# Two cached-attention decodes: spreading the query broadcast over the heads, loading one weight later, and turning the output projections round

## Chip, cores, metric

One core of one Trainium2 chip. The metric is the device time of one execution in microseconds (us); times quoted for a kernel are medians of its runs. A ratio is the mean time of one kernel's fast runs over that of the other's in the same rounds, so it is not quite the ratio of the medians. The kernel before has runs near 883.5 and runs near 886.3 and little between; why, I don't know, and 3 us of any comparison with it are worth no more than that. Differences between two variants are therefore read off their own medians (each was always timed beside the kernel before, on one chip per session).

## The reference

```python
# twice: A with all 16384 keys, B with the last W = 4096 keys
q = (x @ wq).reshape(B, Sq, 32, 128)            # x: 1 x 1 x 512
scores = einsum("bhqd,bhkd->bhqk", q, k) * 128 ** -0.5
o = einsum("bhqk,bhkd->bhqd", softmax(scores), v)
out = o.reshape(B, Sq, 4096) @ wo               # wo: 4096 x 512
# result: concatenate([a, b], axis=-1): 1 x 1 x 1024, bf16
```

One query, 32 heads of 128, each with its own K and V: 352 MB are read and each number is used once.

## The kernel before

Heads alternate: A0, B0, A1, B1, ... (A head i is `hh` = 2i, B head i is `hh` = 2i + 1). K streams through a ring of five slots on the SP queue, V through a ring of four on the ACT queue; a head of A takes two slots, one of B half of one. For A, PE transposes K in groups of eight tiles, ACT copies each group to SBUF, PE multiplies it with q. For B, DVE multiplies K with a q broadcast over all partitions (`qb_sb`) and sums. Both take exp on ACT; PE then multiplies with V, one head later (`ov`).

```python
# SP: a slot is loaded again when its last user is done
if seq[phh][0] == "A": sp.wait_ge(pe_tr, gstart_u[pu] + ugroups[pu])
else:                  sp.wait_ge(dve_red, b_rank[phh] + 1)
...
if hh == WOA_AFTER_HEAD:                        # 6
    sp.wait_ge(pe_q, 1 + 8)                     # all qb batches made: wbuf is free
    sp.dma_start(wo_view[:, :, :], A_wo.rearrange("(c p) n -> p c n", p=128)).then_inc(s_w, 16)

# PE at head 2: broadcast q of B for all heads, eight batches through one PSUM bank
for bch in range(8):
    if bch >= 1: pe.wait_ge(dve_m, DM_QB0 + bch - 1)
    ...  # 16 matmuls of 128 columns into misc7
# DVE: the eight copies stand ahead of its head loop
for bch in range(8):
    v.wait_ge(pe_q, 2 + bch)
    v.tensor_copy(qb_sb[:, bch * 4 * DH : (bch + 1) * 4 * DH], misc7[:, 0 : 4 * DH]).then_inc(dve_m, 1)
for hh in range(NH):
    if hh == last_a_hh + 1: a_final_dve()       # A's tail, ahead of B head 31
    ...

# ACT at a B head: the exp stands ahead of the next A head's copies
act.wait_ge(dve_red, hb + 1)

# PE, the end: 32 matmuls of N = 512 for each branch (b_final likewise, with wob_view)
for h in range(HQ):
    last = pe.matmul(outA_ps, onorm[:, h : h + 1], wo_view[:, h, :], start=(h == 0), stop=(h == HQ - 1))
```

`wo_view` shares its SBUF buffer with wq, so A_wo can only be loaded when the last qb batch is made. B_wo goes into two slots of the K ring, when K is done with them. Both are read as `(c p) n -> p c n`: 32 pieces of 1 KB to a partition, 4096 in all.

The softmax here doesn't subtract the row's maximum and nothing guards it: scores larger than these inputs give would overflow.

## Time and profile before

| | |
|---|---|
| time | 886.31 us, median of the first 6 runs |
| span of the profiled run | 884.8 us |
| bytes read | 352.32 MB, 398 GB/s over the span |
| busy share | PE 73%, weight loads 64%, ACT 56%, DVE 25% |

No engine is near full; the table alone doesn't say what binds. The row of GB/s does: it stands near 424 in most slices. So I kept one ledger: add up, over stretches of 5 us, how much of each stretch the DMA would not have needed at 424 GB/s. A stretch at 212 GB/s has lost 2.5 us. The prediction shows the lines for the kernel before.

### The profile page before, as it was taken

The numbers are of one execution on the slowest core, as the hardware profiler recorded it, in microseconds if no ns is written. First come the engines' busy times: TensorE is split into PE (matmuls) and PEld (weight loads), VectorE is DVE, ScalarE is ACT, GpSimd is POOL, SyncE is SP. The second block draws the span as 40 slices with busy tenths as digits, with TensorE's granted clock in tenths as the row PEclk, the third lists the DMA queues.
The fourth block names the chain that finished last, engine by engine and source line by source line (L and its number), as shares of the span: only waits on it lengthen the run. The fifth ranks groups of instructions, "written<-read, shape, count | busy, mean of one in ns | idle before, by whom it ended". The sixth has DMA issues, their size and how long they took to land.

```text
span 884.8 us, 29291 instructions
## 1 busy us (share of the span) xinstructions
PE 647.1 (73%) x13764; PEld 568.8 (64%) x13764; DVE 223.9 (25%) x87; ACT 498.2 (56%) x641; POOL 0.7 (0%) x6
## 2 busy tenths in 40 slices
PE   0776983687777778777777787777777877767788
PEld 0666872576666667666666676766666766666673
DVE  0016300633321133333211333333112333332003
ACT  0514771575555676655555776555556775555560
POOL 0000000000000000000000000000000000000000
PEclk9955885687667788776678788666688777667788
DMA  8997899999999999999999999999999999999990
GB/s 339 423 428 313 348 408 401 428 423 423 423 426 423 426 423 424 420 417 422 410 425 410 414 426 424 424 414 419 418 419 424 411 416 424 423 408 420 403 337 6
DMA packets 38202, 354.21 MB, mean 400 GB/s; under 512 B 4289, under 2 KB 12481, under 8 KB 12482
## 3 DMA queue, kind: packets, MB, share of 16 engines
q1 hardware_dynamic: 24258, 184.56, 50.8%
q10 hardware_dynamic: 13824, 167.78, 45.1%
q8 instruction: 108, 1.77, 0.8%
q14 instruction: 12, 0.10, 0.0%
HBM read 352.32 MB, written 0.00 MB: 398 GB/s over the span
## 4 chain that ended last, share of the span: by engine, by line
DMA 71%; PE 14%; another core or an unknown queue 7%; DVE 3%; ACT 3%; issue 1%; SPq 1%; ACTq 0%; DVEq 0%
DMA vring<-in_A_v_cache_dram 68%; PE ol L506 7%; DMA kring<-in_A_k_cache_dram 3%; ACT kts L392 3%; PE ktp L470 2%; PE misc L453 2%; DVE sbb L334 2%; PE misc L535 1%; PE misc L557 1%; DVE prd L325 1%; PE sba L486 1%; DVE qb_sb L294 1%; DMA kring<-in_B_k_cache_dram 1%; SPq L214 1%
## 5 line engine op out<-in xcount | busy, mean ns | idle before, releaser
L392 ACT ACTIVATE kts<-ktp 128x1024 bf16<-128x1024 bf16 x512 | 475.0, 1078 | 35.1 <-PE ktp L470 34.5
L470 PE MATMUL ktp<-ident,kring 128*128 128x128 bf16 x4096 | 361.1, 245 | 19.8 <-DMA kring<-in_A_k_cache_dram 19.7
L470 PEld LDWEIGHTS ktp<-ident,kring 128*128 128x128 bf16 x4096 | 285.8, 111 | 21.3 <-DMA kring<-in_A_k_cache_dram 18.4
L486 PE MATMUL sba<-qT_sb,kts 128*128 128x1 bf16 x4096 | 183.2, 166 | 70.6 <-ACT kts L392 42.7
L506 PE MATMUL ol<-ebuf,vring 128*128 128x1 bf16 x5120 | 149.7, 165 | 112.2 <-DMA vring<-in_A_v_cache_dram 107.9
L486 PEld LDWEIGHTS sba<-qT_sb,kts 128*128 128x128 bf16 x4096 | 149.2, 99 | 128.0 <-ACT kts L392 126.8
L506 PEld LDWEIGHTS ol<-ebuf,vring 128*128 128x128 bf16 x5120 | 142.5, 103 | 116.4 <-DMA vring<-in_A_v_cache_dram 110.1
L325 DVE TENSOR_TENSOR prd<-kring,qb_sb 128x4096 bf16<-128x4096 bf16 x32 | 73.3, 2292 | 539.3 <-DMA kring<-in_B_k_cache_dram 539.1
L417 ACT ACTIVATE ebuf<-sbb 128x32 bf16<-128x32 f32 x32 | 7.3, 229 | 319.2 <-PE ol L514 248.1
L334 DVE TENSOR_REDUCE sbb<-prd 128x32 f32<-128x4096 bf16 x32 | 141.4, 4420 | 1.1
L432 PE MATMUL misc<-xT_sb,wbuf 128*128 128x1 bf16 x128 | 3.6, 165 | 25.3 <-DMA wbuf<-in_A_wq_dram 25.3
L432 PEld LDWEIGHTS misc<-xT_sb,wbuf 128*128 128x128 bf16 x128 | 3.5, 104 | 25.3 <-issue 25.3
L453 PE MATMUL misc<-wbuf,xrep 128*128 128x128 bf16 x128 | 15.1, 312 | 5.5 <-DVE qb_sb L294 5.5
L453 PEld LDWEIGHTS misc<-wbuf,xrep 128*128 128x128 bf16 x128 | 13.0, 146 | 7.4 <-DVE qb_sb L294 7.4
L402 ACT ACTIVATE ebuf<-sba 128x128 bf16<-128x128 f32 x32 | 8.9, 277 | 14.4 <-PE sba L486 14.4
L294 DVE CAST qb_sb<-misc 128x512 bf16<-128x512 f32 x8 | 5.5, 692 | 37.2 <-PE misc L453 37.2
L514 PE MATMUL ol<-rowsum,ones_col 128*1 128x1 f32 x128 | 12.1, 164 | 0.0
L300 DVE RECIPROCAL linv<-ol 1x32 f32<-1x32 f32 x1 | 0.3, 346 | 39.9 <-PE ol L514 39.9
L535 PE MATMUL misc<-wbuf,onorm 128*1 128x512 bf16 x32 | 9.7, 478 | 0.5 <-DVE onorm L308 0.5
L557 PE MATMUL misc<-kring,onorm 128*1 128x512 bf16 x32 | 8.8, 442 | 0.5 <-DVE onorm L351 0.5
L535 PEld LDWEIGHTS misc<-wbuf,onorm 128*1 128x1 bf16 x32 | 3.1, 100 | 6.8 <-issue 3.9
L557 PEld LDWEIGHTS misc<-kring,onorm 128*1 128x1 bf16 x32 | 2.9, 94 | 5.9 <-issue 2.5
(25 smaller groups left out, 25.1 us busy)
## 6 DMA issues: line engine op xcount, KB each, us to landing
vring<-in_A_v_cache_dram ACTq DMA_DIRECT2D x64, 2048.0 KB, 23.1
kring<-in_A_k_cache_dram SPq DMA_DIRECT2D x64, 2048.0 KB, 25.1
kring<-in_B_k_cache_dram SPq DMA_DIRECT2D x32, 1024.0 KB, 18.6
vring<-in_B_v_cache_dram ACTq DMA_DIRECT2D x32, 1024.0 KB, 16.4
wbuf<-in_A_wq_dram SPq DMA_DIRECT2D x1, 4096.0 KB, 19.7
wbuf<-in_B_wq_dram SPq DMA_DIRECT2D x1, 4096.0 KB, 20.9
wbuf<-in_A_wo_dram SPq DMA_DIRECT2D x1, 4096.0 KB, 61.7
kring<-in_B_wo_dram SPq DMA_DIRECT2D x1, 4096.0 KB, 37.0
```

The source lines that it names most:

```text
L294: v.tensor_copy(qb_sb[:, bch * 4 * DH : (bch + 1) * 4 * DH], misc7[:, 0 : 4 * DH],).then_inc(dve_m, 1)
L325: v.tensor_tensor(PRD[:, :].rearrange("p (c d) -> p c d", d=DH), Kring[:, ks * UC : ks * UC + TB, :], qb_bcast(hb), op=ALU.mult,).then_inc ...
L334: v.tensor_reduce(SBB[hb % 2][:, 0:TB], PRD[:, :].rearrange("p (c d) -> p c d", d=DH), AXX, ALU.add,).then_inc(dve_red, 1)
L392: act.activation(KTs[g % NS][:, 0 : GS * 128], KTP[g % NKB][:, 0 : GS * 128], ACTF.Copy,).then_inc(act_ev, 1)
L402: act.activation(Ebuf[e][:, 0:TA], SBA[:, 0:TA], ACTF.Exp, bias=0.0, scale=inv_sqrt_dh, accum_out=rowsum[e][:, 0:1],).then_inc(act_ex, 1)
L453: last = pe.matmul(misc7[:, i * DH : (i + 1) * DH], xrep[:, jc, :], wq_view[:, jc, hb * DH : (hb + 1) * DH], start=(jc == 0), stop=(jc == ...
L470: last = pe.transpose(KTP[g % NKB][:, t * 128 : (t + 1) * 128], Kring[:, ks * UC + c, :], ident[:, :],)
L486: last = pe.matmul(SBA[:, c0 + c : c0 + c + 1], KTs[g % NS][:, t * 128 : (t + 1) * 128], qT_sb[:, a_rank[hh] : a_rank[hh] + 1], start=True ...
L506: pe.matmul(OL[b][:, hidx : hidx + 1], Vring[:, vs * UC + c, :], Ebuf[e][:, c0 + c : c0 + c + 1], start=first, stop=(c0 + c == T - 1),)
L514: pe.matmul(OL[b][0:1, HQ + hidx : HQ + hidx + 1], ones_col[:, 0:1], rowsum[e][:, 0:1], start=True, stop=True,).then_inc(pe_ov, 1)
L535: last = pe.matmul(outA_ps, onorm[:, h : h + 1], wo_view[:, h, :], start=(h == 0), stop=(h == HQ - 1),)
L557: last = pe.matmul(outB_ps, onorm[:, HQ + h : HQ + h + 1], wob_view[:, h, :], start=(h == 0), stop=(h == HQ - 1),)
```

## The change

Its intent: keep the start from stopping (the qb batches spread over heads 2, 4, ... 16, their copies put where they are needed), and shorten the serial end (128 matmuls of N = 1 in place of 32 of N = 512, for each branch). A_wo has to be loaded later for the first; A's tail on DVE goes behind B head 31 for the second.

```diff
-            WOA_AFTER_HEAD = 6
+            WOA_AFTER_HEAD = 24
 # DVE
-                for bch in range(8):
+                def qb_copy(bch):
...
                 for hh in range(NH):
-                    if hh == last_a_hh + 1:
-                        a_final_dve()
...
+                    if hb == 0:
+                        qb_copy(0)
+                    if 3 <= hb <= 9:
+                        qb_copy(hb - 2)
...
-                if NH <= last_a_hh + 1:
-                    a_final_dve()
+                a_final_dve()
...
-                v.tensor_copy(out_sb[0:1, 0:D], outA_ps).then_inc(dve_m, 1)
                 v.wait_ge(pe_fin, 4)
-                v.tensor_copy(out_sb[0:1, D : 2 * D], outB_ps).then_inc(
+                v.tensor_copy(out_colsb[:, 0:8], outcol_ps).then_inc(dve_m, 1)
+                v.wait_ge(pe_fin, 5)
+                v.tensor_copy(out_rowsb[0:8, 0:128], outrow_ps).then_inc(
 # PE
-                    if hh == 2:
-                        qb_batches()
+                    if hh >= 2 and hh % 2 == 0 and hh // 2 <= 8:
+                        qb_batches(hh // 2 - 1)
...
-                    for h in range(HQ):
-                        last = pe.matmul(
-                            outA_ps,
-                            onorm[:, h : h + 1],
-                            wo_view[:, h, :],
+                    for nb in range(4):
+                        for h in range(HQ):
+                            last = pe.matmul(
+                                outcol_ps[:, nb : nb + 1],
+                                wo_view[:, h, nb * 128 : (nb + 1) * 128],
+                                onorm[:, h : h + 1],
... # the same for B, then
+                    pe.wait_ge(dve_m, DM_OUTCOL)
+                    pe.transpose(outrow_ps, out_colsb[:, 0:8], ident[:, :]).then_inc(
```

The output is then stored as 8 rows of 256 B in place of one of 2 KB.

More of the change, by code (lines that the diff above doesn't have):

```diff
@@ L141, in bass_concat_heads__gqa_block_cached__sliding_block_cached__decode_kernel @@
         onorm = sbuf("onorm", [128, 2 * HQ], BF16)
-        out_sb = sbuf("out_sb", [1, 2 * D], BF16)
+        out_colsb = sbuf("out_colsb", [128, 8], BF16)
+        out_rowsb = sbuf("out_rowsb", [8, 128], BF16)
         wq_view = wbuf[:, :].rearrange("p (jc n) -> p jc n", jc=NJ)
@@ L159, in bass_concat_heads__gqa_block_cached__sliding_block_cached__decode_kernel @@
         qT_ps = misc6[:, 0:HQ]
-        outA_ps = misc6[0:1, 0:512]
-        outB_ps = misc7[0:1, 0:512]
+        outcol_ps = misc6[:, 0:8]
+        outrow_ps = misc7[:, :].bitcast(BF16)[0:8, 0:128]
         s_x = sem("s_x")
@@ L188, in bass_concat_heads__gqa_block_cached__sliding_block_cached__decode_kernel @@
         DM_ONORMB = 21
-        DM_OUTA = 22
-        DM_OUTB = 23
+        DM_OUTCOL = 22
+        DM_OUTROW = 23
         with nc.Block() as block:
@@ L270, in _ @@
                 ).then_inc(s_w, 16)
-                sp.wait_ge(dve_m, DM_OUTB)
+                sp.wait_ge(dve_m, DM_OUTROW)
                 sp.dma_start(
-                    out[0, 0:1, 0 : 2 * D],
-                    out_sb[0:1, 0 : 2 * D],
+                    out[0, 0, 0 : 2 * D].rearrange("(r c) -> r c", c=128),
+                    out_rowsb[0:8, 0:128],
                 ).then_inc(s_out, 16)
@@ L356, in _ @@
                 ).then_inc(dve_m, 1)
-                v.wait_ge(pe_fin, 2)
-                v.tensor_copy(out_sb[0:1, 0:D], outA_ps).then_inc(dve_m, 1)
                 v.wait_ge(pe_fin, 4)
-                v.tensor_copy(out_sb[0:1, D : 2 * D], outB_ps).then_inc(
+                v.tensor_copy(out_colsb[:, 0:8], outcol_ps).then_inc(dve_m, 1)
+                v.wait_ge(pe_fin, 5)
+                v.tensor_copy(out_rowsb[0:8, 0:128], outrow_ps).then_inc(
                     dve_m, 1
@@ L427, in _, with qT_A_block, qb_batches @@
             def _(pe):
-                pe.wait_ge(s_x, 16 * 2 * NJ)
-                pe.wait_ge(s_w, 16)
-                for ha in range(HQ):
-                    for jc in range(NJ):
-                        ins = pe.matmul(
-                            qT_ps[:, ha : ha + 1],
-                            wq_view[:, jc, ha * DH : (ha + 1) * DH],
-                            xT_sb[:, jc : jc + 1],
-                            start=(jc == 0),
-                            stop=(jc == NJ - 1),
-                        )
-                ins.then_inc(pe_q, 1)
+                def qT_A_block():
+                    pe.wait_ge(s_x, 16 * 2 * NJ)
+                    pe.wait_ge(s_w, 16)
+                    last = None
+                    for ha in range(HQ):
+                        for jc in range(NJ):
+                            last = pe.matmul(
+                                qT_ps[:, ha : ha + 1],
+                                wq_view[:, jc, ha * DH : (ha + 1) * DH],
+                                xT_sb[:, jc : jc + 1],
+                                start=(jc == 0),
+                                stop=(jc == NJ - 1),
+                            )
+                    last.then_inc(pe_q, 1)
+                    pe.wait_ge(dve_m, DM_QTA)
+                qT_A_block()
                 pe.wait_ge(gps, 2)
-                pe.wait_ge(dve_m, DM_QTA)
-                def qb_batches():
+                def qb_batches(b0):
                     pe.wait_ge(s_w, 32)
                     pe.wait_ge(dve_m, DM_XREP)
-                    for bch in range(8):
+                    for bch in range(b0, b0 + 1):
                         if bch >= 1:
@@ L533, in a_final @@
                     last = None
-                    for h in range(HQ):
-                        last = pe.matmul(
-                            outA_ps,
-                            onorm[:, h : h + 1],
-                            wo_view[:, h, :],
-                            start=(h == 0),
-                            stop=(h == HQ - 1),
-                        )
+                    for nb in range(4):
+                        for h in range(HQ):
+                            last = pe.matmul(
+                                outcol_ps[:, nb : nb + 1],
+                                wo_view[:, h, nb * 128 : (nb + 1) * 128],
+                                onorm[:, h : h + 1],
+                                start=(h == 0),
+                                stop=(h == HQ - 1),
+                            )
                     last.then_inc(pe_fin, 1)
@@ L555, in b_final @@
                     last = None
-                    for h in range(HQ):
-                        last = pe.matmul(
-                            outB_ps,
-                            onorm[:, HQ + h : HQ + h + 1],
-                            wob_view[:, h, :],
-                            start=(h == 0),
-                            stop=(h == HQ - 1),
-                        )
+                    for nb in range(4):
+                        for h in range(HQ):
+                            last = pe.matmul(
+                                outcol_ps[:, 4 + nb : 5 + nb],
+                                wob_view[:, h, nb * 128 : (nb + 1) * 128],
+                                onorm[:, HQ + h : HQ + h + 1],
+                                start=(h == 0),
+                                stop=(h == HQ - 1),
+                            )
                     last.then_inc(pe_fin, 1)
+                    pe.wait_ge(dve_m, DM_OUTCOL)
+                    pe.transpose(outrow_ps, out_colsb[:, 0:8], ident[:, :]).then_inc(
+                        pe_fin, 1
+                    )
                 lag = []
```

## The prediction

> **What bounds the kernel now.** I read the page's slices first, then the stretches in which the DMA share falls, then the timeline of the end, and only then the groups and waits. The slices' last two rows:
>
> ```profile
> DMA  8997899999999999999999999999999999999990
> GB/s 339 423 428 313 348 408 401 428 423 423 423 426 423 426 423 424 420 417 422 410 425 410 414 426 424 424 414 419 418 419 424 411 416 424 423 408 420 403 337 6
> HBM read 352.32 MB, written 0.00 MB: 398 GB/s over the span
> ```
>
> Each slice is 884.8 / 40 = 22.1 us. From slice 7 to slice 37 the core reads 403 to 428 GB/s with its DMA engines busy: the bound there is the bytes. At 421 GB/s, 352.3 MB take 837 us, so about 48 us of the span are not full DMA time. They lie in slices 3 and 4 (66 to 110 us), in the last two slices, and a little at the very start. Time saved in the middle on PE, ACT or DVE is worth nothing; time saved in those places is worth its full length, if nothing else then lets the DMA run dry.
>
> The hole near the start, by stretches (us, then busy time and count of PE, PEld, DVE, ACT, POOL, clock, DMA share, GB/s):
>
> ```profile
> 70.00:75.00 5.00, 3.68 (x35) 3.41 (x32) 3.81 (x3) 0.00 (x0) 0.00 (x0) 0.50 1.02 434
> 75.00:80.00 5.00, 0.17 (x6) 0.18 (x7) 4.87 (x2) 1.46 (x4) 0.00 (x0) 0.50 0.44 147
> 80.00:85.00 5.00, 5.00 (x79) 5.00 (x77) 4.97 (x2) 5.00 (x6) 0.00 (x0) 0.50 0.87 370
> 85.00:90.00 5.00, 4.73 (x100) 4.06 (x97) 0.38 (x1) 4.96 (x7) 0.00 (x0) 0.96 0.61 215
> 90.00:95.00 5.00, 3.58 (x92) 2.99 (x91) 4.82 (x2) 4.10 (x7) 0.00 (x0) 1.00 0.46 131
> 95.00:100.00 5.00, 5.00 (x146) 4.95 (x145) 1.89 (x1) 0.68 (x3) 0.00 (x0) 0.57 0.98 419
> ```
>
> From 75 to 95 us the core read (147 + 370 + 215 + 131) x 5 us = 4.32 MB, which is 10.2 us at 425 GB/s: **9.8 us are lost**. Why it ran dry stands in the timeline of the SP queue (start and duration, us; the issue is held for 34.6 us) and then in the chain that ended last:
>
> ```profile
> 44.24 34.62 SPq L234 DMA_DIRECT2D kring<-in_A_k_cache_dram  x2
> ```
>
> ```profile
> 71.77 2.29 DVE prd L325
> 74.08 4.43 DVE sbb L334
> 78.77 1.01 ACT kts L392
> ```
>
> The second of these two K loads needs the slot of B head 0, which is free only when DVE has reduced it (78.5 us). DVE reduces it only after all eight qb copies, because they stand ahead of the head loop; PE makes the eight batches in one lump from 50.5 to 71 us, 2.67 us each (1.9 matmul, 0.7 copy). ACT also waits there, its exp of B head 0 standing ahead of head 2's evictions; so the SP queue and the V loads both stop.
>
> The end, in the timeline:
>
> ```profile
> 860.07 0.35 DVE L300 RECIPROCAL linv<-ol 1x32 f32<-1x32 f32 x1 [39.91 <-PE ol L514]
> 861.61 9.75 PE L535 MATMUL misc<-wbuf,onorm 128*1 128x512 bf16 x32 [0.51 <-DVE onorm L308]
> 871.29 0.95 PE L506 MATMUL ol<-ebuf,vring 128*128 128x1 bf16 x32
> 872.40 0.35 DVE L343 RECIPROCAL linv<-ol 1x32 f32<-1x32 f32 x1 [4.18 <-PE ol L514]
> 873.72 8.75 PE L557 MATMUL misc<-kring,onorm 128*1 128x512 bf16 x32 [0.51 <-DVE onorm L351]
> 882.51 0.68 DVE L360 CAST out_sb<-misc 1x512 bf16<-1x512 f32 x1 [8.26 <-PE misc L557]
> 883.21 0.32 SPq L272 DMA_DIRECT2D out_dram<-out_sb  x1
> ```
>
> From 860 us to the end it is one serial chain with no DMA left to hide behind. The two output projections are 18.5 of its 24.7 us.
>
> **What the Trainium skill says.** (1) "DMA: Bandwidth & Descriptors", section "Issuing engines are not separate DMA queues": loads issued from SP and ACT run on the same 16 engines. The trace agrees: both queues are active, yet the sum stays near 424 GB/s. (2) "TensorE: Matmul & The Clock Gate", section "Back-to-back issue gap": a matmul of N=512 follows the last after N/1.2 ns cold, N/2.4 + 2.5 ns warm (427 and 216); the section before it puts a floor of about 25 ns on any matmul, however small N is. In the trace the weight loads of line 535 start 0.42 to 0.43 us apart while the clock is 0.50, so that agrees; and the N=1 matmuls, each with its own 128-column weight load, come at 149.7 us / 5120 = 29.2 ns, near the floor. (3) The first page's "Specifications" say that below 512 B the DMA does a read-modify-write. The new output store has 256 B rows; no row of this trace shows what eight of them cost.
>
> **The change, part by part.**
>
> 1. *qb batches spread over heads 2, 4, ... 16, with the copies moved into DVE's loop.* Same count of instructions; it moves them. Only batch 0 stays ahead of B head 0: PE has it at 52.4 us, the copy ends at 53.1, product and sum take 2.3 + 4.4 us, so B head 0 is reduced at 60.0 instead of 78.5. The stopped K load leaves at 60 instead of 78.9. I follow the issues on. Head 2's first K unit lands at 58.1 (issued 29.35, 28.7 us), so its evictions start at 60 and free its slot about 66.8 (6.6 us later, as before): one more 1 MiB load. Its second unit lands near 68 and is done near 75: 2 MiB of K, then 1 MiB of V for head 3. B head 1 (landed 73.4) is reduced at about 80.1: 2 MiB of K. The V units of head 4 follow near 78 and 81: 4 MiB. Before, 29 MiB had been issued when the DMA ran dry at 76. Now 3 MiB more are in by 67, good to 83.5 us at 2.5 us per MiB; and 9 MiB more are in by 81, good to about 106. After that PE and ACT need about 23 us a pair of heads against the DMA's 25.1 us, so the queues stay filled. Gain: the whole 9.8 us, less some residue: **9.5 us**. The later batches add 1.9 us to PE in eight pairs of heads, in a stretch where PE waits for V anyway: 0.
>
> 2. *A_wo loaded after head 24 instead of 6.* It must move, since wq's buffer is now in use until head 16. Same 4 MiB, same 1 KB pieces. Before, it took 61.7 us to land and held K back until PE stood still (140 to 160 us), yet the DMA stayed at 420 to 424 GB/s there, with one dip to 360 in 130 to 140 (1.5 us). The same should happen near 300 us: 0.
>
> 3. *Projections with wo as the stationary operand.* Each 32 matmuls of N=512 become 4 x 32 = 128 of N=1. 128 x 29.2 ns = 3.74 us against 9.75 and 8.75. Gain 6.0 + 5.0 = **11.0 us**, all on the chain. The next wait below is B_wo, issued at 828.0 with 37.0 us to landing, so at 865.0. The new chain is at its B projection at 861.61 + 3.74 + 0.95 + about 1.4 = 867.7: 2.7 us to spare.
>
> 4. *New end.* Instead of a 0.68 us cast of 1x512: a 128x8 copy (0.2), a transpose (0.3 with its wait), an 8x128 copy (0.2) and hand-overs (0.05 each), about 0.85 in all. Cost **0.2 us**, and perhaps 0.1 more for the store in eight rows.
>
> 5. *DVE's A tail after B head 31 instead of before.* B head 31's product and sum leave 861.5 to 868.2 us and run near 840, when K has landed. They were hidden under A's projection, but under the new 3.7 us one they would not have been: this part alone gains 0, and without it part 3 would lose about 3 us.
>
> Sum: -9.5 - 11.0 + 0.3 = -20.2 us: 886.3 becomes 866.1.
>
> **The rivals.** (a) *The early hole closes only in part or opens again later.* Against it: the issue times above have more than 20 us in hand by 81 us. For it: they are chained by hand, and the first-in-first-out K queue may hold one unit back. It would leave 3 to 6 us of the hole: 869 to 872. (b) *B_wo becomes the wait at the end.* Its margin is 2.7 us, and in the last 10 us before landing it moves under 220 GB/s. If it lands late, part 3 loses 1 to 3 us: 867 to 869. (c) *The late A_wo load opens a hole of its own* when the V ring is full and K stands behind 4 MiB of 1 KB pieces. Against: the same load behind the same depth of rings left the DMA full before. It would cost 2 to 5 us: 868 to 871. (d) *Only the tail counts*, the start being made up by rings that refill: not so, as in the middle the DMA is at its rate and nothing can be caught up or lost; it would give 875.
>
> **Range and chances.** The central value is 866.0. Runs of the kernel before spread by 3 us, the tail is sure to about 1 us, the start to 3 us, mostly upward, and (b) and (c) also go upward. The line of 2% is 868.6, only 2.6 us above. Range 862.5 to 871; faster by over 2% 0.79, within 2% 0.20, slower 0.01.
>
> **What would show it.** Slices 3 and 4 at 415 GB/s or more; the K load that the SP queue held 34.6 us gone at about 60 us; no stretch of 5 us before 800 us under 350 GB/s. Each projection 3.5 to 4 us; from the first reciprocal of the tail to the store about 12.5 us instead of 23.1; B's projection started by the onorm product and not by the B_wo load. A_wo landing near 300 us or later with the DMA share above 0.95 around it. I would be wrong if a stretch between 60 and 110 us still shows a hole, if the DMA share dips about A_wo's load, or if N=1 matmuls over wo come slower than 30 ns.

## The result, and the profile after

867.09 us (866.54 to 867.40, 8 runs) against 886.31: ratio 0.9792, 95% interval 0.9778 to 0.9806. The result is correct. Repeated in another session, 866.77 us and 0.9796. The interval spans 0.98, so whether the gain is over 2% is not settled.

The slices of the changed kernel (span 865.3 us, so 21.6 us each):

```profile
DMA  8999999999999999999999999999999999999993
GB/s 339 423 426 424 424 428 423 423 426 424 422 422 426 424 424 408 358 421 409 423 428 420 427 424 425 423 423 412 417 417 425 425 419 420 413 412 417 412 397 125
```

The dent in slices 3 and 4 is gone, and the last slice no longer stands at 6 GB/s. A new dent is in slices 15 to 18 (325 to 411 us). The start in two views, the SP queue's timeline and a stretch (same columns as in the prediction):

```profile
44.21 16.13 SPq L235 DMA_DIRECT2D kring<-in_A_k_cache_dram  x2
65.81 0.33 SPq L235 DMA_DIRECT2D kring<-in_B_k_cache_dram  x1
```

```profile
75.00:95.00 20.00, 18.57 (x408) 16.67 (x409) 6.47 (x3) 13.09 (x18) 0.00 (x0) 0.83 1.01 426
```

The second of the two K loads now ends its issue at 44.21 + 16.13 = 60.3 us, where it was 78.9, and the 20 us that had lost 9.8 run at 426 GB/s.

The new dent, in the timeline of the SP queue and in stretches:

```profile
303.21 0.68 SPq L251 DMA_DIRECT2D wbuf<-in_A_wo_dram  x1
314.05 52.77 SPq L235 DMA_DIRECT2D kring<-in_B_k_cache_dram  x1
```

```profile
355.00:360.00 5.00, 0.00 (x0) 0.00 (x0) 0.00 (x0) 0.00 (x0) 0.00 (x0) 0.50 1.04 439
360.00:365.00 5.00, 0.00 (x0) 0.00 (x0) 0.00 (x0) 0.00 (x0) 0.00 (x0) 0.50 0.71 295
365.00:370.00 5.00, 0.00 (x0) 0.00 (x0) 0.00 (x0) 0.00 (x0) 0.00 (x0) 0.50 0.80 266
370.00:375.00 5.00, 0.00 (x0) 0.00 (x0) 0.19 (x1) 0.00 (x0) 0.00 (x0) 0.50 1.06 438
```

A_wo is issued at 303 us, and the issue of the next K load, a single instruction, takes 52.77 us. By 355 us no engine has anything to do, and from 360 to 370 the DMA itself is not full.

The end, in the timeline:

```profile
850.65 0.34 DVE L301 RECIPROCAL linv<-ol 1x32 f32<-1x32 f32 x1 [15.62 <-PE ol L520]
852.19 1.30 PE L542 MATMUL misc<-onorm,wbuf 128*128 128x1 bf16 x43 [0.51 <-DVE onorm L309]
854.34 2.40 PE L542 MATMUL misc<-onorm,wbuf 128*128 128x1 bf16 x85 [0.85 <-issue]
857.75 0.35 DVE L345 RECIPROCAL linv<-ol 1x32 f32<-1x32 f32 x1 [5.63 <-PE ol L520]
859.30 3.57 PE L565 MATMUL misc<-onorm,kring 128*128 128x1 bf16 x128 [0.51 <-DVE onorm L353]
863.13 0.27 PE L574 MATMUL misc<-ident,out_colsb 128*8 128x128 bf16 x1 [0.26 <-DVE out_colsb L360]
863.67 0.36 SPq L273 DMA_DIRECT2D out_dram<-out_rowsb  x1
```

From the first reciprocal to the end it was 24.7 us and is 14.7. The projections take 4.6 us (with a pause of 0.85 for which the trace shows no releaser) and 3.6 us.

The ledger of the two profiled runs, us lost against 424 GB/s:

| stretch | before | after |
|---|---|---|
| 0 to 50 us | 4.4 | 4.3 |
| 50 to 100 us (qb lump) | 9.7 | -0.1 |
| around the A_wo load (before 100 to 150, after 300 to 400) | 1.8 | 5.1 |
| the rest up to 800 us | 5.8 | 3.2 |
| 800 us to the end | 27.7 | 17.3 |

So 9.8 us came from the start and 10.4 from the end, and 3.3 were given back around A_wo. The fourth row differs by 2.6 us for no reason that I can show. Together the rows give 19.6 us; the two spans differ by 19.5.

### The profile page after: what moved, and what is told of

The parts are those of the page before. It is cut to its first block, busy times and chain, and to the rows that moved or that the text cites. A ratio compares the mean times of both kernels' runs of the same rounds, so it can differ in the third digit from the quotient of the medians.

```text
span 865.3 us, 29684 instructions
## 1 busy us (share of the span) xinstructions
PE 633.0 (73%) x13957; PEld 565.0 (65%) x13957; DVE 222.5 (26%) x87; ACT 498.2 (58%) x641; POOL 0.7 (0%) x6
## 4 chain that ended last, share of the span: by engine, by line
DMA 77%; PE 12%; another core or an unknown queue 5%; ACT 2%; DVE 2%; issue 2%; SPq 1%; ACTq 0%; DVEq 0%
DMA vring<-in_A_v_cache_dram 66%; PE ol L512 7%; DMA kring<-in_A_k_cache_dram 4%; DMA kring<-in_B_k_cache_dram 4%; DMA wbuf<-in_A_wq_dram 2%; ACT kts L394 2%; PE ktp L476 2%; DVE sbb L337 1%; PE sba L492 1%; DVE prd L328 1%; SPq L215 0%; PE ol L520 0%; PE misc L542 0%; PE misc L565 0%
## 5 line engine op out<-in xcount | busy, mean ns | idle before, releaser
L476 PE MATMUL ktp<-ident,kring 128*128 128x128 bf16 x4096 | 356.1, 243 | 33.6 <-DMA kring<-in_A_k_cache_dram 33.6
L476 PEld LDWEIGHTS ktp<-ident,kring 128*128 128x128 bf16 x4096 | 282.4, 110 | 34.9 <-DMA kring<-in_A_k_cache_dram 32.7
L492 PEld LDWEIGHTS sba<-qT_sb,kts 128*128 128x128 bf16 x4096 | 147.2, 98 | 128.0 <-ACT kts L394 126.9
L404 ACT ACTIVATION_READ_ACCUMULATOR ebuf<-sba 128x1 f32 x32 | 6.2, 194 | 0.0
L520 PEld LDWEIGHTS ol<-rowsum,ones_col 128*1 128x1 f32 x128 | 5.5, 80 | 1.0
L419 ACT ACTIVATION_READ_ACCUMULATOR ebuf<-sbb 128x1 f32 x32 | 6.0, 186 | 0.0
L542 PE MATMUL misc<-onorm,wbuf 128*128 128x1 bf16 x128 | 3.7, 165 | 1.4 <-issue 0.8
L542 PEld LDWEIGHTS misc<-onorm,wbuf 128*128 128x128 bf16 x128 | 3.6, 104 | 1.6 <-issue 0.9
(27 smaller groups left out, 14.7 us busy)
## 6 DMA issues: line engine op xcount, KB each, us to landing
kring<-in_B_wo_dram SPq DMA_DIRECT2D x1, 4096.0 KB, 36.5
```

Source lines behind the costliest of these rows:

```text
L404: act.activation(Ebuf[e][:, 0:TA], SBA[:, 0:TA], ACTF.Exp, bias=0.0, scale=inv_sqrt_dh, accum_out=rowsum[e][:, 0:1],).then_inc(act_ex, 1)
L419: act.activation(Ebuf[e][:, 0:TB], SBB[hb % 2][:, 0:TB], ACTF.Exp, bias=0.0, scale=inv_sqrt_dh, accum_out=rowsum[e][:, 0:1],).then_inc(act ...
L476: last = pe.transpose(KTP[g % NKB][:, t * 128 : (t + 1) * 128], Kring[:, ks * UC + c, :], ident[:, :],)
L492: last = pe.matmul(SBA[:, c0 + c : c0 + c + 1], KTs[g % NS][:, t * 128 : (t + 1) * 128], qT_sb[:, a_rank[hh] : a_rank[hh] + 1], start=True ...
L520: pe.matmul(OL[b][0:1, HQ + hidx : HQ + hidx + 1], ones_col[:, 0:1], rowsum[e][:, 0:1], start=True, stop=True,).then_inc(pe_ov, 1)
L542: last = pe.matmul(outcol_ps[:, nb : nb + 1], wo_view[:, h, nb * 128 : (nb + 1) * 128], onorm[:, h : h + 1], start=(h == 0), stop=(h == HQ ...
```

## The experiments

All but e8, e9 and e10 produce the right result. Medians:

| label | what it is | us |
|---|---|---|
| (changed) | | 867.09, again 866.77 |
| e1_tail_only | new end only | 876.39 |
| e2_lump_wo24 | changed, qb lump back | 876.18 |
| e3_final_first | changed, A's tail on DVE first | 869.60 |
| e4_wo_4pieces | changed, A_wo in 4 pieces | 863.01 |
| e5_b0_early | lump back, B head 0 ahead of the other copies | 874.18 |
| e6_lump_late | lump at head 6 | 872.57 |
| e7_wo_16pieces | changed, A_wo in 16 pieces | 862.44 |
| e8_wo_long_rows | changed, A_wo in long rows | 860.62 |
| e9_before_long_rows | before, A_wo in long rows | 881.53 |
| e10_lump_long_rows | e2 with long rows | 872.10 |
| e12_wo_halves | e7, B_wo in two halves | 862.77 |

(e11_changed_again is the control.)

### Which part gives what: e1 and e2

```diff
 # e2: on the changed kernel               # e1: the same, and
+ for bch in range(8):  (all copies ahead of the loop)
- if hb == 0: qb_copy(0)                    - WOA_AFTER_HEAD = 24
- if 3 <= hb <= 9: qb_copy(hb - 2)          + WOA_AFTER_HEAD = 6
+ if hh == 2: for b0 in range(8): qb_batches(b0)
```

> The changed kernel with the qb lump and the early A_wo load of the kernel before put back, so that only the new projections, the new end and the later A tail on DVE remain. My theory (start and tail gain separately, and the DMA rate between them is fixed): the tail alone gains 10 to 11 us, 886.3 becomes about 876; the early hole from 75 to 95 us is there again with about 9.7 us lost. Rival (the rings make up a stop at the start, only the tail counts): 867 to 869.

> The same with A_wo after head 24, so that it differs from the tail-only kernel in the place of this load alone, and from the changed kernel in the qb lump alone. If a late A_wo load costs nothing (as I predicted): same as the tail-only kernel, about 876. If the hole seen in the changed kernel at 360 to 370 us comes from the late place (the changed kernel loses 5.1 us around that load against 424 GB/s, the kernel before 1.8): 3 us slower than the tail-only kernel, about 879. If the lost time at the start is a matter of A_wo not yet being queued, more than that, 882 or over.

Measured 876.39 (875.81 to 877.14) and 876.18 us (875.45 to 876.88). The end alone is worth 9.4 us against the kernel before of the same session (885.76). The spread is worth the distance from e2 to the changed kernel, 9.1 us; so it isn't made up by the rings, as one rival had it. And the place of the A_wo load is worth nothing in a kernel that still has the lump. That speaks against my reading of the trace before this run, 3 us for the late place; the next runs show where that comes from.

### The order on DVE: e3

```diff
                 for hh in range(NH):
+                    if hh == last_a_hh + 1:
+                        a_final_dve()
...
-                a_final_dve()
                 v.wait_ge(pe_ov, NH)
```

> The changed kernel with the A tail on DVE put back ahead of B head 31's product and sum. My theory: those 6.7 us are hidden under A's projection only when it takes 9.75 us, so PE waits for the exp of head 31 after the new one: 2.5 to 3 us slower than the changed kernel, about 869.8. Rival (the order on DVE is of no account, as the K of head 31 is late): same as the changed kernel, 867.

Measured 869.60 us (869.39 to 869.94): 2.5 to 2.8 us slower. Where work is hidden only because its neighbour is slow, speeding up the neighbour exposes it; the change was right to move it as well.

### Which wait stopped the start: e5 and e6

```diff
 # e5, on the changed kernel: PE's eight batches at head 2; DVE:
                     if hb == 0:
                         qb_copy(0)
-                    if 3 <= hb <= 9:
-                        qb_copy(hb - 2)
+                    if hb == 1:
+                        for b1 in range(1, 8):
+                            qb_copy(b1)
 # e6: PE batch 0 at head 2, batches 1 to 7 at head 6; DVE:
+                    if hb == 3:
+                        for b1 in range(1, 8):
+                            qb_copy(b1)
```

> The changed kernel with PE's eight qb batches back in one lump at head 2, but DVE doing B head 0 right after copy 0 and copies 1 to 7 only then. The stopped K load leaves at 60 us as in the changed kernel. If the slot of B head 0 was the binding wait at the start (as I wrote in the prediction): near 867. If the lump on PE binds in its place (batch 2 waits for copy 1, so the lump now ends near 75 us, head 2's evictions start near 77 and the next loads leave near 90): the hole moves to about 81 to 91 us and is only 1 to 2 us smaller than with the whole lump; about 874 to 875.

Measured 874.18 us (873.98 to 874.60), as expected for the lump on PE. The stopped K load leaves as early as in the changed kernel, and the hole is still there, moved to 80 to 95 us:

```profile
44.40 16.19 SPq L235 DMA_DIRECT2D kring<-in_A_k_cache_dram  x2
83.03 0.33 SPq L235 DMA_DIRECT2D kring<-in_B_k_cache_dram  x1
```

```profile
75.00:80.00 5.00, 5.00 (x59) 5.00 (x57) 3.38 (x3) 2.57 (x3) 0.00 (x0) 0.52 1.01 426
80.00:85.00 5.00, 4.62 (x101) 3.86 (x99) 3.92 (x1) 5.00 (x7) 0.00 (x0) 1.00 0.36 111
85.00:90.00 5.00, 4.52 (x93) 3.67 (x94) 2.05 (x1) 5.00 (x6) 0.00 (x0) 1.00 0.42 175
90.00:95.00 5.00, 3.78 (x121) 3.38 (x119) 4.66 (x2) 2.57 (x5) 0.00 (x0) 0.85 0.73 272
```

The load after it now leaves at 83.0, against 65.8 in the changed kernel. So the wait that the SP queue showed was one of two, and freeing the slot does not bring the 9.1 us. The 2.0 us that e5 gains over e2 are no clean share of the slot, though: because DVE now reduces B head 0 between copies 0 and 1, the lump itself ends later, at 76.5 us where it ends at 71.8 in e2. What moves by 2.0 us is the start of head 2's copies on ACT: 79.4 us in e2, right after the exp of B head 0; 77.4 in e5, after the lump; 60.2 in the changed kernel. In the kernel before they start at 78.8 although PE's lump ended at 71.1: there they waited for the exp of B head 0, and so for DVE, which had to make all eight copies first. How the 9.1 us divide between PE's lump and this order on DVE and ACT is not shown, as e5 takes away the second but lengthens the first.

> The changed kernel with batch 0 at head 2 and batches 1 to 7 in one lump of about 19 us at head 6, their copies just before B head 3. If what a stop of PE costs is only what the DMA queues cannot bridge, and they hold some 9 to 10 MiB (22 to 25 us) by then: 867 to 869, with at most 2 us of DMA time lost from 100 to 140 us. If a lump costs its length less PE's slack wherever it stands: 875 or over.

Measured 872.57 us (871.62 to 873.67): a miss, 3.6 us over the first theory and 2.4 under the second. The queues did bridge their 25 us: the last V load before the stop was issued at 106 us, and the DMA ran full to 130. But the stop was longer than the lump. K is asked for again only when a slot (half a head of A) has been transposed: the lump ends at 124, ACT starts on head 6 at 125, and the first free slot comes at 130.7, the next at 138.0:

```profile
94.85 6.31 SPq L235 DMA_DIRECT2D kring<-in_A_k_cache_dram  x2
130.71 0.33 SPq L235 DMA_DIRECT2D kring<-in_B_k_cache_dram  x1
138.04 0.81 SPq L235 DMA_DIRECT2D kring<-in_A_k_cache_dram  x2
```

```profile
125.00:130.00 5.00, 4.91 (x86) 4.74 (x85) 4.96 (x2) 4.91 (x6) 0.00 (x0) 0.73 0.96 403
130.00:135.00 5.00, 4.52 (x95) 3.67 (x93) 1.59 (x1) 5.00 (x6) 0.00 (x0) 1.00 0.79 293
135.00:140.00 5.00, 3.49 (x71) 2.63 (x69) 3.66 (x2) 4.89 (x6) 0.00 (x0) 1.00 0.23 57
140.00:145.00 5.00, 4.01 (x144) 3.87 (x144) 3.05 (x1) 0.37 (x2) 0.00 (x0) 0.64 0.97 405
```

The ledger gives 6.0 us lost from 100 to 150. So the cost is not the lump's length less what is queued: the queue lasts to 130, but then one request of 1 MiB, at 130.7, has to do until 138.0.

### What the A_wo load costs: e4, e7, e8, e9, e10

```diff
 # e4: after heads 24, 26, 28, 30, c_w = 8; e7: after heads 17, 19, ... 47, c_w = 2
+                        sp.dma_start(
+                            wo_view[:, i_w * c_w : (i_w + 1) * c_w, :],
+                            A_wo.rearrange("(c p) n -> p c n", p=128)[
+                                :, i_w * c_w : (i_w + 1) * c_w, :
+                            ],
 # e8, e9, e10: wrong weights on purpose, the same bytes to the same place
-                            A_wo.rearrange("(c p) n -> p c n", p=128),
+                            A_wo.rearrange("(p c) n -> p c n", p=128),
```

> The changed kernel with A_wo loaded in four pieces of 1 MiB after heads 24, 26, 28 and 30. If the loss around the load (5.1 us against 424 GB/s) is the K queue standing still behind 4096 pieces of 1 KB until the V ring is full: the hole at 360 to 370 us goes, no K issue takes over 20 us, and the time falls by 3 to 4 us to about 863.5. If it is the poorer rate of 1 KB pieces whatever stands around them: the time stays at 866 to 867.

> The changed kernel with the same 4 MiB of A_wo in the same place, but read so that each partition takes 32 KB that lie together, in place of 32 pieces of 1 KB. The output of the first half is wrong on purpose; the work is the same. If the loss around the load is a matter of the 1 KB pieces (their number fills the K queue's ring so that the next K load cannot be issued for 52.8 us): the hole at 360 to 370 us is gone, no K issue is held over 20 us, 862 to 863. If it is 4 MiB standing ahead of K, whatever their pieces: the hole stays, 867.

> The changed kernel with A_wo in 16 pieces of 256 KB after heads 17, 19, ... 47. Four pieces gave 863.0 and still lost some 3 us around the load. If that is the K queue behind its 1 KB pieces, finer and wider spread pieces lose less: 860.5 to 862.5. If the 1 KB pieces themselves move more slowly at whatever spread, the loss is only spread too: 863.

Measured 863.01 (e4), 860.62 (e8) and 862.44 us (e7). The same 4 MiB in the same place, in rows of 32 KB, save 6.3 us (mean of the two medians of the changed kernel, 866.9, less 860.6): it is the form of the load, not the 4 MiB ahead of K, and the gain is larger than either theory of e8 gave. Four loads instead of one win 3.9 of them, sixteen 4.5. Long rows also change the order in which the weights are read; but e4 and e7 keep the pieces and their order and win most of the gain, so that rival can account for little.

e4's time is as expected, its sign is not: the K issue behind each of its four loads still took 15.4 to 21.6 us, and 3.1 us are still lost from 300 to 400 us. In e7 no K issue is held any more (0.33 to 0.47 us behind each load); its time lies on the edge between its two theories and doesn't decide. It is 1.8 us over e8, so what the 1 KB pieces cost without a held queue is some 1.8 of the 6.3 us or less: an estimate from these two runs, whose loads also stand at different times (and e7 waits 2.1 us longer for B_wo at its end).

The issue of the K load behind A_wo shows it best. In the kernel before it took 30.9 us, behind long rows 0.33, at the same moment (SP queue's timeline, the kernel before first, then e9):

```profile
105.26 30.89 SPq L234 DMA_DIRECT2D kring<-in_B_k_cache_dram  x1
```

```profile
105.19 0.33 SPq L234 DMA_DIRECT2D kring<-in_B_k_cache_dram  x1
```

The load cut into 4096 pieces keeps the queue from taking the next one until late in its own time (136.2 us; A_wo lands at 92.7 + 61.7 = 154.4). That some list of pieces is full is my inference. That the form of the load does it, these two lines show; that it is the number of pieces in one load, e4 and e7 show: pieces of the same 1 KB, 1024 to a load, hold the next K issue for 15.4 to 21.6 us, and 256 do not hold it.

> The kernel before with only A_wo read in long rows (4 MiB in the same place, output of the first half wrong on purpose). In the changed kernel long rows saved 6.5 us. If the 1 KB pieces cost the same wherever the load stands, as my prediction of 0 for its move implies: 879.5 to 880. If the early place among emptier queues was cheaper (the trace of the kernel before loses only 1.8 us around it): 883 to 885.

> The changed kernel with the qb lump at head 2 and A_wo after head 24 in long rows (wrong on purpose in the first half). Against the changed kernel with long rows (860.6) it gives the worth of the spread batches without the A_wo load in the way. By the hole in the trace, 9.7 to 10.2 us: 870.5 to 871. If the spread is worth only the 9.1 us that the runs with 1 KB pieces show: 869.7; if the pieces hid more of it, over 872.

Measured 881.53 (e9) and 872.10 us (e10); the control e11 in the same session 866.77.

> The changed kernel itself, on the same chip as the two others, as a control: 867 and a ratio of about 0.979.

e9 is 4.2 us under the kernel before by the means of their runs, between what the two theories gave; the interval of its ratio, 0.9931 to 0.9977, makes that 2 to 6 us. e10 came out as its third case, over 872. With it there is a square:

| | 1 KB pieces | long rows | the pieces cost |
|---|---|---|---|
| lump | 876.18 (e2) | 872.10 (e10) | 4.1 |
| spread | 866.9 (changed) | 860.62 (e8) | 6.3 |
| the spread gives | 9.3 | 11.5 | |

The pieces cost 4.1 to 4.2 us in the kernels with the lump, early (e9) or late (e10), and 6.3 in the changed one. So the late place costs nothing by itself, as e1 and e2 had said, but the spread and the pieces get in each other's way for 2.2 us (roughly 1 to 3, as the four runs of e2 lie 1.4 us apart). In the traces the held K issue is 30.9 us in the kernel before, 32.7 in e2 and 52.8 in the changed kernel. That the held issue is longer because the rings are fuller when it comes fits this, but no run varies it alone. The ledger accounts for 9.9 of the 11.5 us of the last row in the hole at 50 to 100 us; the rest is spread over the middle and stays open.

### Once A_wo is out of the way: e12

In e4, e7 and e8 the end has a new wait, here in the waits of e7 (engine, line, waited for: us in total, times, longest):

```profile
PE misc L570 <- DMA kring<-in_B_wo_dram: 4.0, 1, 4.0
```

```diff
 # e12, on e7: for each of the two slots, as soon as it is free
+                    sp.dma_start(
+                        wob_view[:, c_b : c_b + 16, :],
+                        B_wo.rearrange("(c p) n -> p c n", p=128)[:, c_b : c_b + 16, :],
```

> The kernel with A_wo in 16 pieces, and B_wo loaded in two halves, each as soon as its own K slot is free, in place of one load when both are. With 16 pieces the B projection waited 4.0 us for B_wo, which was issued at 818.9 us, when B head 30 was reduced; the first slot was free some 8 us earlier. If that wait is the end's bound: the first half leaves near 811, the wait shrinks by 2 to 4 us and the time is 859 to 860.5. If the DMA is full there anyway, so that the half that goes earlier only delays the V loads on which the A tail waits: 862 to 863.

Measured 862.77 us (862.50 to 863.15), no gain: the wait is 3.4 us instead of 4.0, and A's tail starts a good microsecond later. Of the two theories, the number fits the second, but its cause is another. The first half went out at 811.0 us, but the issue of the second alone took 24.06 us: again 1 KB pieces held the queue, and the DMA fell to 286 GB/s, where e7 has 389 (SP queue's timeline, then a stretch):

```profile
818.86 24.06 SPq L274 DMA_DIRECT2D kring<-in_B_wo_dram  x1
```

```profile
830.00:840.00 10.00, 8.39 (x217) 7.32 (x213) 1.95 (x1) 7.80 (x10) 0.00 (x0) 0.92 0.74 286
```

So 2048 pieces held the issue behind them too. This cause is read from the trace alone; B_wo in long rows was not tried. The best correct kernels are e7 and e4, both 0.9745 of the kernel before (0.9728 to 0.9762 and 0.9730 to 0.9760), some 4 us under the changed one, with e12 (0.9746) beside them.

## Why the prediction was right

It said 866.0 us; it is 867.1, inside the range, and a gain of 2.1% where 2.3% was foreseen. By its steps:

1. **The spread of the qb batches** (predicted 9.5): 9.1 to 9.3 by e2. The hand-worked times hold within 1 us: the K load at 60.3 (60), the next at 65.8 (66.8), then 74.0 (75) and 80.5 (80.1), B head 0 reduced at 55.56 + 4.42 = 60.0 (60.0). What it named first, the slot of B head 0, is not enough: e5 frees it and gets 2.0 us in all. The start of head 2's copies, held by the order on DVE and ACT or by the lump on PE, which it named second, has to come earlier as well. And that 9.5 was met so closely is partly luck: with A_wo out of the way the spread gives 11.5 us (e10 against e8), 1.6 of them outside the hole that was counted, and the pieces take 2.2 back.
2. **The late A_wo load** (predicted 0): as a term by itself right (0.2 us, e1 against e2), so the sum 9.3 + 0.2 + 9.4 = 18.9 comes near the 19.2 us measured. But "the same should happen near 300 us" was wrong, and two of the signs that the prediction set itself went against it: the DMA share falls to 0.71 and 0.80 from 360 to 370 us, with 295 and 266 GB/s where no stretch was to be under 350. The K issue there is held for 52.8 us instead of 30.9, the ledger loses 5.1 us instead of 1.8, and by the square 2.2 us of what the spread could give are lost. It is rival (c) with its lower figure of 2 us. The trace of the kernel before had the clue, an issue of 30.89 us, and I had read past it because the DMA stayed full there.
3. **The projections and the new end** (predicted 11.0 - 0.3 = 10.7): 9.4 by e1, 10.1 in the trace from the first reciprocal on. B's took 3.57 us (3.74); A's took 4.6, more than the 4 that was set, because of the pause of 0.85 us. From the first reciprocal to the store it is 13.0 us (12.5). From the last projection's end to the store it is 0.8 us, as worked out. The kernel before's two groups of runs keep the rest from being settled.
4. **A's tail behind B head 31** (predicted: without it about 3 us lost): 2.5 to 2.8 by e3.
5. **Rival (b)**, B_wo as the wait at the end: not in the changed kernel. It lands at 818.8 + 36.5 = 855.3, and the B projection starts at 859.3. It comes true once A_wo is cheaper (e4, e7, e8: 2.7, 4.0 and 1.9 us).
6. **Rivals (a) and (d)**: no hole before 300 us, and e2 shows that the start counts.

The pace of the N = 1 matmuls, on which step 3 rests, was confirmed: 3.57 us / 128 = 27.9 ns for one with its weight load.

## What to carry to other kernels

Where DMA is the bound, look for the stretches in which it isn't full, and work each saving out as the DMA time it gives back; then follow the requests forward until the queue is full again, because freeing the one wait that the queue shows may free only the first of two (e5). A load in many small pieces costs more than its bytes: it can hold the queue for everything behind it, so cut it into several loads and spread them, even when its place in time seems harmless. And when a stage is made faster, check what it had been hiding (e3) and what comes next behind it (B_wo in e7).

## What the Trainium skill lacked or had wrong

- "DMA: Bandwidth & Descriptors", "Issuing engines are not separate DMA queues", calls the time to initiate a DMA "usually small relative to the DMA itself". Here a K load of 1 MiB took 30.9 us to issue behind 4 MiB in 1 KB pieces, 52.8 in the changed kernel, and 0.33 us behind the same bytes in 32 KB rows; behind 1 MiB in 1024 pieces of 1 KB it took 15.4 to 21.6 us (e4), behind 256 pieces 0.33 to 0.47 (e7). The page's section "Queues, rings and completion order" gives no number of pieces from which a queue holds its issuer.
- The same page, "Specifications", sets 512 B as the least size for the full rate. 1 KB pieces are above it, and a load of 4 MiB in them cost 4.1 us (lump) and 6.3 us (spread) of the whole time more than in long rows. In e7, where no K load is held, some 1.8 of the 6.3 us or less are left (an estimate from e7 and e8), so the larger part goes with the held queue.
- No page that I read has the pause of 0.85 us, without a releaser, within a run of 128 matmuls that all their operands stand ready for (0.84 or 0.85, always before the last 85 of them, in every profile with the new end and A_wo in one load; none in e4, e7 and e12).
